# Attention beside a Fourier transform on one core: six tiles of exponentials instead of seven, and the turn of the maxima in another burst

## The chip, the cores and the metric

The kernel runs on one core of a Trainium2 chip. A core has a matrix engine (TensorE, in the profile PE, its weight loads PEld), VectorE (DVE), ScalarE (ACT), GpSimd (POOL) and SyncE (SP), which here only issues DMAs. The time is that of one execution on the device, in microseconds (us); "before" is the median of three runs.

## The reference

`x` is 2048 x 640, all in float32.

```python
g = sigmoid((x * gate_w).sum(-1, keepdims=True))
# a: attention with 32 heads of 20
q, k, v = split(x @ wqkv)
a = softmax(q @ k.T * 20 ** -0.5) @ v            # per head
a = merge_heads(a) @ wo
# b: Fourier mixing, real part
b = dft_seq_re @ (x @ dft_hid_re.T) - dft_seq_im @ (x @ dft_hid_im.T)
out = g * a + (1 - g) * b
```

## The kernel before

Attention is cut into 32 units: 16 pairs of heads by two halves of the queries. A unit has 32 steps, 1024 steps in all. Step `i` takes 128 keys and 512 queries for both heads of the pair: two score matmuls on PE ("e", transposed scores, into a PSUM bank each), two exponentials on ACT (L1123) into one tile `[128, 2, 512]`, and later the products with V on PE (L739), which add into the bank `av`. Softmax needs each query's maximum beforehand. So PE also computes plain scores ("m", L201), 43 steps ahead, and DVE reduces them (L203). When a unit's last m is done, `max_nm` (L218) makes the negated maxima `nm`, and `turn_max` transposes them on PE (L239), splits them on DVE into `m`, stores that to `m_scr` (L244) and loads it as two more rows of the queries `qst` (L250), so that the maxima are subtracted inside the e matmul. Store and load are handed to SP at the start of a step (`at_step`): 1 and 3 steps later.

The steps are grouped in cycles, and a table of letters sets PE's order inside a cycle: e and m are scores, F is a share of the other work (the Fourier transforms and the output product), B is the burst, in which the V products of all steps of the cycle run back to back. There are 56 cycles of 4 steps with the hidden transform; then the sequence transform (56 units of PE work, 672 steps), in which six of every eight units stand over two cycles of 6 steps (table `THIRDS`, "long") and two over three cycles of 4 (`SEQUENCE`, "short"), so 84 long and 42 short ones; then cycles of 4 with the output product. A unit of attention is 32 steps, so the ends of units recur in a pattern of 96 steps, 18 cycles.

The last pair of e in a cycle belongs to the first step of the next one. So a long cycle has seven live tiles of exponentials before its burst: five `p` buffers (`pair_tile`), one tile `p2`, and one lent by the pool `raw` of three buffers, which holds data from DRAM for POOL to split. The two extra tiles stand in `spares` and are taken in turn, two of every seven steps. In the sequence transform `raw` holds the chunks of the DFT matrix (`load_c`, L679, two of them at times; a second operand goes to `raw2`), which POOL adds (L685) and splits (L135, L136) into `part`; in the last of the seven products also a slab of the output weights (`wos`, L835).

All engines follow an order written by this program, in order; SP also issues its DMAs in order, so one that waits holds those behind it. PSUM banks for scores are five, taken in turn by `bank()`. An `E` in a table is an e whose score is computed at its place, but whose exponential (and whose step's start, `begin`) is kept in `held` until the burst's first product has been issued. `burst` also runs up to two of the queued `extras` (reading out a finished transform, adds, stores).

Of the kernel before, what the change touches and what calls it, by code (L numbers as in the profile page):

```python
# [34 lines left out]

HIDDEN = "emeFFmeFFFmeFFFmeFFmeFeFFFmFemmB", {"e": (0, 0, 1, 1), "m": (1, 1, 0, 1)}
SEQUENCE = "emeFmFFFFemFeFFmeFFemFFFmmFFFmeeB", {"e": (0, 0, 1, 1), "m": (1, 1, 1, 1)}
THIRDS = "emFemeFFFFmeFFmFeFmFFeFmeFFFmeFFmeFFmeFFFmFmmFeeB", {"e": (0, 1, 0, 1, 0, 1), "m": (1, 0, 1, 0, 1, 1)}
OUTPUT = "emFeFmFemeFFmeFFmeFFmFmFeFmeB", {"e": (1, 0, 0, 1), "m": (0, 1, 1, 0)}
LATE = "eeeeFFFFFFeeeEB", {"e": (0, 0, 0, 0), "m": (0, 0, 0, 0)}  # L40

# [52 lines left out]
def mix_kernel(ctx: ExitStack, tc: tile.TileContext, xa, xh, wqk, wb, wr, cdft, wo, out):  # L94
# [4 lines left out]
    def pools(**kw):  # L99
        return ctx.enter_context(tc.tile_pool(**kw))  # L100
# [44 lines left out]
    def bank():  # L145
        return ps_w.tile([P, 512], F32, name=f"ps{free[0][next(turn) % len(free[0])]}")
# [6 lines left out]
    def pair_tile():  # L153
        return work.tile([P, 2, 512], F32, name="p", bufs=5)

    def raw_tile():
        return work.tile([P, 1024], F32, name="raw", bufs=3)
# [8 lines left out]
    def load_stack(p):  # L166
        for t, o, parts in ((kst[p % 2], D, (0, 1, 0)), (qst[p % 2], 0, (0, 0, 1))):
            for h in range(2):
                r = o + (2 * p + h) * DH
                for k, z in enumerate(parts):  # L170
                    b = 64 * h + k * DH
                    yield (f32(t[b : b + DH, :]).rearrange("r (t c) -> r t c", t=4),
                           qk_scr[z, :, r : r + DH, :].rearrange("t r c -> r t c"))

    def q_unit(n):
        u = n % 2 * (S // 2)
        return qst[n // 2 % 2][:, u : u + S // 2]

    steps = [0]
    mx, nms, ends = {}, {}, []  # L180
# [6 lines left out]
    def at_step(i, fn):  # L187
        later.setdefault(i, []).append(fn)


    def s_mm(i, h):
        n, s = divmod(i, 32)
        if n >= NU:
            return lambda: None
        qt, kc = divmod(s, 4)
        q, k = q_unit(n), kst[(n // 2) % 2]
        if n not in mx:
            mx[n] = small.tile([P, 2, 8, 4], F32, name="mx", bufs=2)
        ps = bank()
        b = 64 * h  # L200
        pe.matmul(ps, q[b : b + KROWS, qt * P : (qt + 1) * P],  # L201
                  k[b : b + KROWS, kc * 512 : (kc + 1) * 512], start=True, stop=True)
        return lambda: dve.tensor_reduce(mx[n][:, h, qt, kc : kc + 1], ps, axis=AX.X, op=ALU.max)  # L203

    def s_end(i):
        n, s = divmod(i, 32)
        if n < NU and s == 31:
            if now[0] < 0:
                max_nm(n)
            else:  # L210
                ends.append(n)
        if s == 1 and 0 < n <= NU and now[0] < 0:
            turn_max(n - 1)

    def max_nm(n):
        nms[n] = small.tile([P, 32], F32, name="nm", bufs=2)
        m = mx.pop(n).rearrange("p h q (o c) -> p o (h q) c", o=1).to_broadcast([P, 2, 16, 4])
        dve.tensor_reduce(nms[n].rearrange("p (o k) -> p o k", o=2), m, axis=AX.X, op=ALU.max, negate=True)  # L218
# [118 lines left out]
    def flush(keep=0):  # L337
        while len(stores) > keep:
            sp.dma_start(*stores.pop(0))
# [329 lines left out]
    cparts, pts = {}, {}  # L669
# [63 lines left out]
    def av_step(i, n, kt):  # L733
        v = vts[n // 2]
        pp = [pts.pop((n, kt, qc)) for qc in range(2)]
        for qc in range(2):
            for h in range(2):
                j = 2 * qc + h
                pe.matmul(av[32 * j : 32 * j + DH + 1, :], v[:, kt, h * (DH + 1) : (h + 1) * (DH + 1)],  # L739
                          pp[qc][:, h, :], start=kt == 0, stop=kt == NS - 1)  # L740
        if kt == NS - 1:
            unit_end(i, n)
# [195 lines left out]
    def run_extras(g, most):  # L938
        while extras and most and extras[0][0] <= now[0]:
            extras.pop(0)[1]()  # L940
            most -= 1
        if more(g):
            n = g // (HT * NS) + 1
            preps.append((now[0] + 4, load_a(n, made.setdefault(n, 0))))
            made[n] += 1
        if preps and preps[0][0] <= now[0]:
            preps.pop(0)[1]()
# [7 lines left out]
    def start_dft():  # L955
        flush()
        wide.release()
        apool.append(pools(name="apool", bufs=1))
        spares.append(raw_tile().rearrange("p (z c) -> p z c", z=2))
        spares.append(apool[0].tile([P, 2, 512], F32, name="p2"))  # L960
        make_sel()
    ops = {}
# [2 lines left out]
    def make_sel():  # L965
        sel = apool[0].tile([P, P], F32, name="sel")
        for j in range(4):
            c = 32 * j + DH
            pool.tensor_copy(sel[:, 32 * j : 32 * j + 32], ident[:, c : c + 1].to_broadcast([P, 32]))
        chain.append(sel)  # L970
# [16 lines left out]
    HID = 8 * len(FEATURE)  # L987
# [9 lines left out]
    for u in range(UNITS):  # L997
        c = len(steps) - 1
# [7 lines left out]
    for u in range(2 * len(PRE)):  # L1006
        n = 2 if u >= 2 * len(PRE) - SLOW else 1
# [6 lines left out]
    def plan(c):  # L1014
        if HID <= c < outs_at:
            return THIRDS if steps[c + 1] - steps[c] == 6 else SEQUENCE
        return LATE if c >= late else OUTPUT if c >= outs_at else HIDDEN
# [9 lines left out]
    for k, tt in enumerate(PRE):  # L1027
        i = steps[tiles[2 * k]]
# [13 lines left out]
    def begin(i):  # L1042
        now[0] = i
        n, s = divmod(i, 32)
        for fn in later.pop(i, ()):
            fn()
        if s % 2 == 0:
            flush()
        if s == 0 and n % 2 == 0:
            p = n // 2  # L1050
            if p + 1 < NP:
                at_step(i + 6, functools.partial(load_v, p + 1))
            if 0 < p < NP - 1:
                for j, args in enumerate(load_stack(p + 1)):
                    at_step(i + 2 + j, functools.partial(sp.dma_start, *args))
        if i < total:
            k = (i - steps[HID]) % 7 - 5
            pts[n, s // 2, s % 2] = spares[k] if k >= 0 and steps[HID] < i <= steps[outs_at] else pair_tile()

    def end(i):  # L1060
        if i % 4 == 2:
# [28 lines left out]
    held, newest, spares = [], [], []  # L1090
    seen_ = const.tile([1, 1], F32, name="seen")

    def score(kind):
        hold, kind = kind == "E", kind.lower()
        x = heads[kind]
        heads[kind] += 1
        i, z = divmod(x, 2)
        h = z
        first, goes = plan(at_cycle[0])[1][kind], x - (2 * LEAD if kind == "m" else 0) - 2 - 2 * steps[at_cycle[0]]
        h ^= first[goes // 2 % len(first)]  # L1100
        if kind == "m":
            s_mm(i, h)()
            if z:
                s_end(i)
            if goes == 9 and len(first) == 6:
                pass_ends()
            return
        if z == 0 and i <= total and not hold:
            begin(i)
        if i < total:  # L1110
            n, s = divmod(i, 32)
            kt, qc = divmod(s, 2)
            q, k = q_unit(n), kst[(n // 2) % 2]
            b = 64 * h
            pt = bank()
            pe.matmul(pt, k[b : b + KROWS + 2, kt * P : (kt + 1) * P],  # L1116
                      q[b : b + KROWS + 2, qc * 512 : (qc + 1) * 512], start=True, stop=True)

            def exp():
                if z == 0 and hold:  # L1120
                    begin(i)
                newest[:] = [pts[n, kt, qc][:, h]]
                act.activation(newest[0], pt, AF.Exp, scale=float(DH) ** -0.5)  # L1123
                if z:
                    end(i)
                if goes == 2 * len(first) - 3:
                    while copies:
                        copies.pop()()

            held.append(exp) if hold else exp()  # L1130

    turned = []

    def pass_ends():
        for n in ends:
            max_nm(n)
        turned.extend(ends)
        ends.clear()

    def burst(c):  # L1140
        run_extras(max(done - HIDS, 0) // 3, 3 if c <= HID else 2)
        for n in ends:
            max_nm(n)
        for kt in range(steps[c] // 2, steps[c + 1] // 2):
            av_step(now[0], kt // NS, kt % NS)
            while turned:
                turn_max(turned.pop(0))
            while held:
                held.pop(0)()
        turned[:] = ends  # L1150
        ends.clear()
        if steps[c + 1] < total:
            act.activation(seen_, newest[0][0:1, 0:1], AF.Copy)
        if c == HID - 1:
            start_dft()
# [142 lines left out]
```

## Time and profile before

| | us |
|---|---|
| median of three runs | 1842.54 |
| lowest, highest | 1838.28, 1844.77 |
| the profiled execution | 1844.79 |
| its span | 1843.0 |
| hidden transform, first burst to last | 235.11 to 573.02 |
| sequence transform | to 1638.68 |
| output product, then the tail | to 1812.60, to 1843.0 |

"Busy" is the time in which an engine executes; time with a wait is not counted. Rows of a timeline give start, duration, engine, line, operation, output <- input, shapes, count, and in brackets the idle time before it with what ended it.

### The profile page before, as it was taken

What the parts mean: (1) busy time and instruction counts of PE and PEld (TensorE: products, weight loads), DVE (VectorE), ACT (ScalarE), POOL (GpSimd) and SP (SyncE); (2) the same over time, 40 slices, a digit from 0 to 9 for tenths busy, and PEclk for the clock granted to TensorE, in tenths of its full rate; (3) what the DMA queues carried; (4) which work ended last, traced back from release to release, by engine and by line L of the source; (5) the groups of instructions that cost most, each with busy time, mean ns of one, the idle gap of its engine ahead of it and who ended that gap; (6) DMA issues with size and microseconds to landing.
All of it is one profiled execution on the core that took longest, in us unless ns stands there. A gap on an engine that the chain in (4) does not pass through costs nothing. (4 is left out here: it accounts for less than half of the span.)

```text
span 1843.0 us, 45446 instructions
## 1 busy us (share of the span) xinstructions
PE 1818.7 (99%) x17917; PEld 1323.8 (72%) x17917; DVE 1425.6 (77%) x2427; ACT 1264.5 (69%) x2590; POOL 1303.7 (71%) x1104
## 2 busy tenths in 40 slices
PE   9999999999997999999999999999999999999998
PEld 7988876767675777777777777777777776676666
DVE  4157489888886888888788888888888887789953
ACT  4233377777775777777677777777777776677786
POOL 1379735666689788557779999967889987824444
PEclk9999999999998999999999999999999999999999
DMA  7899954877775574545576777556485856542224
GB/s 237 193 325 367 330 178 137 229 222 220 243 215 183 181 231 135 149 127 165 179 197 215 205 215 228 166 169 189 149 229 180 238 153 178 173 102 79 63 55 158
DMA packets 196009, 349.60 MB, mean 190 GB/s; under 512 B 54239, under 2 KB 107615, under 8 KB 194003
## 3 DMA queue, kind: packets, MB, share of 16 engines
q1 hardware_dynamic: 194515, 341.45, 61.3%
q0 software_dynamic: 1280, 5.25, 1.3%
q8 instruction: 141, 2.31, 0.5%
q14 instruction: 73, 0.60, 0.1%
HBM read 257.79 MB, written 88.65 MB: 188 GB/s over the span
## 5 line engine op out<-in xcount | busy, mean ns | idle before, releaser
L203 DVE TENSOR_REDUCE mx<-ps 128x1 f32<-128x512 f32 x2048 | 1269.6, 684 | 243.9 <-PE ps L201 208.5
L1123 ACT ACTIVATE p<-ps 128x512 f32<-128x512 f32 x1856 | 993.4, 601 | 359.2 <-PE ps L201 203.5
L201 PE MATMUL ps<-kst,qst 60*128 60x512 f32 x2048 | 747.6, 404 | 12.6 <-ACT raw L1123 9.4
L1116 PE MATMUL ps<-qst,kst 62*128 62x512 f32 x2048 | 717.2, 407 | 4.1 <-DMA qst<-m_scr 4.1
L827 PE MATMUL yp<-x,part 64*128 64x320 f32 x5376 | 661.8, 307 | 0.0
L827 PEld LDWEIGHTS yp<-x,part 64*128 64x128 f32 x5376 | 603.3, 186 | 8.1
L739 PE MATMUL av<-p,v 128*21 128x512 f32 x3712 | 486.5, 598 | 0.0
L1116 PEld LDWEIGHTS ps<-qst,kst 62*128 62x128 f32 x2048 | 340.2, 185 | 199.9 <-issue 77.7
L201 PEld LDWEIGHTS ps<-kst,qst 60*128 60x128 f32 x2048 | 345.8, 184 | 25.9 <-ACT raw L1123 9.7
L136 POOL TENSOR_TENSOR part<-raw,part 128x1024 fp32r<-128x1024 f32 (+3 forms) x134 | 296.7, 2214 | 10.2
L739 PEld LDWEIGHTS av<-p,v 128*21 128x21 f32 x3712 | 98.1, 101 | 202.3 <-issue 193.1
L518 PE MATMUL yp<-wb,x 64*128 64x320 f32 x1680 | 211.4, 306 | 0.0
L685 POOL TENSOR_TENSOR raw<-raw,raw 128x1024 f32<-128x1024 f32 x78 | 188.2, 2413 | 23.6 <-DMA raw<-in_cdft 17.6
L135 POOL CAST part<-raw 128x1024 fp32r<-128x1024 f32 (+2 forms) x127 | 125.0, 984 | 111.3 <-PE yp L827 79.6
L518 PEld LDWEIGHTS yp<-wb,x 64*128 64x128 f32 x1680 | 194.2, 186 | 2.5
L1123 ACT ACTIVATE raw<-ps 128x512 f32<-128x512 f32 x192 | 107.5, 599 | 49.0 <-PE ps L201 25.8
L739 PE MATMUL av<-raw,v 128*21 128x512 f32 x384 | 99.9, 599 | 0.0
L898 PE MATMUL yp<-x,part 64*128 64x320 f32 x720 | 92.5, 311 | 0.0
L531 POOL TENSOR_TENSOR x<-x,raw 128x640 f32<-128x640 f32 x40 | 62.6, 1564 | 41.8 <-DVE raw L528 37.9
L714 POOL TENSOR_TENSOR araw<-araw 128x320 f32<-128x320 f32 x80 | 70.1, 876 | 30.3 <-DMA araw<-a_scr 29.0
L136 POOL TENSOR_TENSOR x<-araw,x 128x320 fp32r<-128x320 f32 x96 | 84.0, 875 | 7.7
L898 PEld LDWEIGHTS yp<-x,part 64*128 64x128 f32 x720 | 80.3, 186 | 1.6
(117 smaller groups left out, 1507.9 us busy)
## 6 DMA issues: line engine op xcount, KB each, us to landing
raw<-in_cdft SPq DMA_DIRECT2D x188, 512.0 KB
araw<-a_scr SPq DMA_DIRECT2D x176, 160.0 KB
qk_scr<-p SPq DMA_DIRECT2D x40, 512.0 KB
kst<-qk_scr SPq DMA_DIRECT2D x90, 160.0 KB
w_scr<-wb SPq DMA_DIRECT2D x36, 400.0 KB
qst<-qk_scr SPq DMA_DIRECT2D x90, 160.0 KB
wb<-w_scr SPq DMA_DIRECT2D x8, 1600.0 KB
part<-in_xh SPq DMA_DIRECT2D x10, 1024.0 KB
```

The costliest lines, as they stand in the source:

```text
L135: e1.tensor_copy(dst1, src)
L136: e2.tensor_tensor(dst2, src, f32(dst1), op=ALU.subtract)
L201: pe.matmul(ps, q[b : b + KROWS, qt * P : (qt + 1) * P], k[b : b + KROWS, kc * 512 : (kc + 1) * 512], start=True, stop=True)
L203: return lambda: dve.tensor_reduce(mx[n][:, h, qt, kc : kc + 1], ps, axis=AX.X, op=ALU.max)
L518: pe.matmul(ps[z], lefts[n][a][r, d, k * P : k * P + P], rights[2 * n + hf][r, b, d], start=done_ == 0, stop=done_ == 3 * ND - 1)
L685: pool.tensor_tensor(raws[0], raws[0], raws[1], op=ALU.add if PRODUCTS[n][0][1][0] > 0 else ALU.subtract)
L714: pool.tensor_tensor(raws[0], raws[0], raws[1], op=ALU.add if PRODUCTS[n][1][1][0] > 0 else ALU.subtract)
L739: pe.matmul(av[32 * j : 32 * j + DH + 1, :], v[:, kt, h * (DH + 1) : (h + 1) * (DH + 1)], pp[qc][:, h, :], start=kt == 0, stop=kt == NS - 1)
L827: pe.matmul(yp[h][:, :HE], c[r, cz, cs], a[r, az], start=s == 0 and z == 0, stop=s == NS - 1 and z == 2)
L898: pe.matmul(yp[h][:, :HE], o[r, oz, d], wos[d, hf][r, wz], start=d == 0 and z == 0, stop=d == ND - 2 and z == 2)
L1116: pe.matmul(pt, k[b : b + KROWS + 2, kt * P : (kt + 1) * P], q[b : b + KROWS + 2, qc * 512 : (qc + 1) * 512], start=True, stop=True)
L1123: act.activation(newest[0], pt, AF.Exp, scale=float(DH) ** -0.5)
```

## The change

The step ahead of a long cycle is no longer exponentiated before that cycle's burst, but inside it, after the first product (the letters `EE`). Six tiles then do: five `p` and `p2`, which is taken at every sixth step; the pool `raw` keeps its three buffers. And a unit's maxima that end in a long cycle are no longer reduced and queued in mid-cycle (`pass_ends`, after the tenth m, if they had ended by then). `burst` reduces them at its start and turns them after its last product; in a short cycle the turn comes in the next burst, as before.

```diff
-THIRDS = "emFemeFFFFmeFFmFeFmFFeFmeFFFmeFFmeFFmeFFFmFmmFeeB", {"e": (0, 1, 0, 1, 0, 1), "m": (1, 0, 1, 0, 1, 1)}
+THIRDS = "emFemeFFFFmeFFmFeFmFFeFmeFFFmeFFmeFFmeFFFmFmmFEEB", {"e": (0, 1, 0, 1, 0, 1), "m": (1, 0, 1, 0, 1, 1)}
...
-        spares.append(raw_tile().rearrange("p (z c) -> p z c", z=2))
         spares.append(apool[0].tile([P, 2, 512], F32, name="p2"))
...
-            k = (i - steps[HID]) % 7 - 5
-            pts[n, s // 2, s % 2] = spares[k] if k >= 0 and steps[HID] < i <= steps[outs_at] else pair_tile()
+            spare_ = steps[HID] < i <= steps[outs_at] and (i - steps[HID]) % 6 == 5
+            pts[n, s // 2, s % 2] = spares[0] if spare_ else pair_tile()
...
-            if goes == 9 and len(first) == 6:
-                pass_ends()
...
-    def pass_ends():
-        for n in ends:
-            max_nm(n)
-        turned.extend(ends)
-        ends.clear()
-
     def burst(c):
         run_extras(max(done - HIDS, 0) // 3, 3 if c <= HID else 2)
         for n in ends:
             max_nm(n)
-        for kt in range(steps[c] // 2, steps[c + 1] // 2):
+        kts = range(steps[c] // 2, steps[c + 1] // 2)
+        if len(kts) > 2:
+            turned.extend(ends)
+            ends.clear()
+        for kt in kts:
             av_step(now[0], kt // NS, kt % NS)
-            while turned:
+            while turned and (len(kts) == 2 or kt == kts[-1]):
                 turn_max(turned.pop(0))
             while held:
                 held.pop(0)()
-        turned[:] = ends
+        turned.extend(ends)
         ends.clear()
```

In the built program three places show it. First ACT's queue at the end of the first long cycle (the numbers behind names tell buffers' uses apart; `o` is the unit's result copied out of `av`). Before:

```order
L1123 ACTIVATE p_8739<-ps0_8752 128x512
L1123 ACTIVATE raw_8654<-ps2_8762 128x512
L1123 ACTIVATE raw_8654<-ps4_8772 128x512
L1128 ACTIVATE o_8646<-av_97 128x512
L1123 ACTIVATE p2_8655<-ps3_8802 128x512
L1123 ACTIVATE p2_8655<-ps4_8805 128x512
L1153 ACTIVATE seen_2691<-p2_8655 1x1
```

And now:

```order
L1120 ACTIVATE p_8738<-ps0_8751 128x512
L1120 ACTIVATE p2_8654<-ps2_8761 128x512
L1120 ACTIVATE p2_8654<-ps4_8771 128x512
L1125 ACTIVATE o_8646<-av_97 128x512
L1120 ACTIVATE p_8814<-ps3_8794 128x512
L1120 ACTIVATE p_8814<-ps4_8796 128x512
L1148 ACTIVATE seen_2691<-p_8814 1x1
```

The sixth step's exponentials go to `p2` instead of the lent `raw`, and the seventh's to a `p` that the burst frees; ACT's order is the same here.

Second PE's queue in a burst that turns a unit's maxima (the fourth long cycle of the sequence transform). Before:

```order
L1116 MATMUL ps1_9278<-qst1_94,kst1_92 128x512
L739 MATMUL av_97<-p_9117,v_6185 21x512 x2
L739 MATMUL av_97<-raw_8654,v_6185 21x512 x2
L239 MATMUL ps2_9294<-ident_86,nm_9261 32x32 x4
L739 MATMUL av_97<-p2_8655,v_6185 21x512 x2
L739 MATMUL av_97<-p_9188,v_6185 21x512 x2
L739 MATMUL av_97<-p_9210,v_6185 21x512 x2
L739 MATMUL av_97<-p_9238,v_6185 21x512 x2
L1116 MATMUL ps3_9313<-qst1_94,kst1_92 128x512
```

And now:

```order
L1113 MATMUL ps1_9275<-qst1_94,kst1_92 128x512
L739 MATMUL av_97<-p_9132,v_6185 21x512 x2
L739 MATMUL av_97<-p_9144,v_6185 21x512 x2
L739 MATMUL av_97<-p_9163,v_6185 21x512 x2
L739 MATMUL av_97<-p_9190,v_6185 21x512 x2
L739 MATMUL av_97<-p_9212,v_6185 21x512 x2
L739 MATMUL av_97<-p2_8654,v_6185 21x512 x2
L239 MATMUL ps2_9303<-ident_86,nm_9286 32x32 x4
L1113 MATMUL ps3_9316<-qst1_94,kst1_92 128x512
```

The four transposes move from behind the first of three products (four matmuls each) to behind the last. In the unit of every three whose last m stands in the last place of a long cycle, they move from this place in the burst after to that in the cycle's own burst. Nothing else in PE's order changes.

Third SP's queue in the last product of the sequence transform, where output weights are loaded too. Before:

```order
L835 DMA raw_24890<-in_wo 128x640
L244 DMA m_scr_85<-m_25018 128x64
L679 DMA raw_25042<-in_cdft 128x1024
L679 DMA raw2_25044<-in_cdft 128x1024
L835 DMA raw_25055<-in_wo 128x640
L769 DMA r_scr_81<-lc_24395 128x16
L931 DMA y_scr_80<-yt_24561 128x320
L250 DMA qst1_94<-m_scr_85 1x32x32 x4
```

And now:

```order
L835 DMA raw_24960<-in_wo 128x640
L931 DMA y_scr_80<-yt_24629 128x320
L244 DMA m_scr_85<-m_25096 128x64
L679 DMA raw_25114<-in_cdft 128x1024
L679 DMA raw2_25116<-in_cdft 128x1024
L835 DMA raw_25127<-in_wo 128x640
L769 DMA r_scr_81<-lc_24462 128x16
L250 DMA qst1_94<-m_scr_85 1x32x32 x4
```

The store of a transform's sum (`y_scr`) stands one step earlier, ahead of the maxima's store; such stores move so in many places, since `burst` counts their eight steps from a step that has not yet begun. The loads keep their order, with three buffers of `raw` to take instead of two.

## The prediction

> **What bounds the kernel now.** I read the page first: who is busy, and what clock TensorE was granted.
>
> ```profile
> PE 1818.7 (99%) x17917; PEld 1323.8 (72%) x17917; DVE 1425.6 (77%) x2427; ACT 1264.5 (69%) x2590; POOL 1303.7 (71%) x1104
> ...
> PEclk9999999999998999999999999999999999999999
> ```
>
> PE is busy for 99% of the span, so no engine but PE sets the time, and a change that leaves PE's instructions alone can win only PE's few idle microseconds and the time spent at a lower clock. The clock dips in the 13th of 40 slices. Next I read whom PE waited for.
>
> ```profile
> PE ps L201 <- ACT raw L1123: 9.4, 1, 9.4
> PE ps L1116 <- DMA qst<-m_scr: 4.1, 3, 2.0
> PE ps L201 <- DMA qst<-qk_scr: 2.7, 1, 2.7
> ```
>
> Five waits, 16.2 us, and each falls in the DFT stage whose buffers the change rearranges. To price them with what follows them, I took stretches of whole cycles (from the start of one AV burst to the start of a later one) that hold a wait, and beside each a stretch with the same place in the repeating pattern of long and short cycles and no wait. Columns: the stretch, its length, busy time (and count) of each engine, granted clock, DMA share, GB/s.
>
> ```profile
> 573.02:602.25 29.23, 19.85 (x187) 13.85 (x185) 15.35 (x26) 13.49 (x27) 25.16 (x24) 0.82 0.58 193
> 640.58:658.25 17.67, 17.67 (x187) 13.23 (x185) 15.02 (x26) 13.58 (x27) 17.09 (x14) 1.00 0.87 243
> 872.80:895.13 22.33, 20.66 (x202) 13.92 (x201) 15.39 (x29) 14.06 (x28) 14.94 (x11) 0.92 0.44 132
> 723.52:742.22 18.70, 18.70 (x203) 13.54 (x201) 15.41 (x29) 14.06 (x28) 10.29 (x9) 1.00 0.56 152
> 1324.39:1334.56 10.17, 9.70 (x106) 6.90 (x104) 8.41 (x17) 6.72 (x14) 7.93 (x7) 1.00 0.50 155
> 723.52:732.91 9.39, 9.39 (x106) 6.83 (x104) 7.64 (x16) 6.70 (x13) 5.62 (x6) 1.00 0.33 90
> 1528.44:1537.02 8.58, 6.62 (x66) 4.61 (x64) 6.32 (x11) 4.45 (x10) 5.95 (x7) 1.00 0.41 119
> 1378.94:1385.20 6.26, 6.26 (x66) 4.43 (x64) 5.06 (x10) 4.44 (x9) 5.97 (x8) 1.00 0.67 187
> 1560.95:1573.29 12.34, 9.67 (x98) 6.91 (x96) 7.99 (x15) 6.89 (x14) 12.04 (x8) 1.00 0.84 244
> 1409.12:1418.40 9.28, 9.28 (x99) 6.71 (x97) 7.81 (x14) 6.89 (x14) 8.99 (x8) 1.00 0.55 168
> ```
>
> The counts of PE agree within one in each pair, so the differences are pure loss: 29.23 - 17.67 = 11.56 us, 22.33 - 18.70 = 3.63, 10.17 - 9.39 = 0.78, 8.58 - 6.26 = 2.32, 12.34 - 9.28 = 3.06. Together 21.35 us. In the first two pairs the loss is larger than PE's idle time in the row (9.38 and 1.67), because the granted clock fell to 0.82 and 0.92. The clean stretches show no idle PE at all, so in steady state nothing is to be won.
>
> **The lent raw tile (term 1, 11.56 us).** The one long wait, engine by engine:
>
> ```profile
> 590.46 0.79 PE L201 MATMUL ps<-kst,qst 60*128 60x512 f32 x1 [9.38 <-ACT raw L1123]
> 589.81 1.09 ACT L1123 ACTIVATE raw<-ps 128x512 f32<-128x512 f32 x2 [9.97 <-POOL part L136]
> 568.50 2.41 POOL L136 TENSOR_TENSOR part<-wb,part 128x1024 fp32r<-128x1024 f32 x1
> 583.92 2.34 POOL L685 TENSOR_TENSOR raw<-raw,raw 128x1024 f32<-128x1024 f32 x1 [2.73 <-DMA raw<-in_cdft]
> 587.44 2.34 POOL L136 TENSOR_TENSOR part<-raw,part 128x1024 fp32r<-128x1024 f32 x1
> ```
>
> The first exponential into the lent tile needs one of three raw buffers; the first to come free holds a DFT matrix chunk, which POOL reads until 587.44 + 2.34 = 589.78, and the exponential starts at 589.81. The PSUM banks stay full behind it and PE stops for want of one. After the change that step goes to the tile `p2`, whose memory POOL last read in the row at 568.50, over at 570.91, ten microseconds before the exponential wants it; the next step is held and takes the tile that the burst's first product releases. Nothing in the first long cycle waits for a raw tile. POOL's add of the last hidden-transform product moves ahead of the chunk's sum, into the 2.73 us in which POOL idles for the chunk's DMA; an add of nearly that size would still fit. Next late is POOL's chunk for the second DFT unit: finished at 589.78 as before, and needed when PE has done the two cycles of the clean row (17.67) and the burst behind them, 573.02 + 17.67 + 2.7 = 593.4. So 3.6 us of cover are left, and I take the whole 11.56; the ends are 11.56 and, if POOL's chain came late by as much as one more chunk (2.34 + 2.34 plus its cast, about 6 us), 9.
>
> **The turn of the maxima (term 2, 3.63 + 0.78 us).** Every third unit's maxima end in the last score pair of a long cycle, too late for the mid-cycle call, and are turned one burst later.
>
> ```profile
> 874.45 0.32 SPq L244 DMA_DIRECT2D m_scr<-m  x1
> 877.92 2.71 SPq L250 DMA_DIRECT2D qst<-m_scr  x4
> 883.61 0.59 PE L1116 MATMUL ps<-qst,kst 62*128 62x512 f32 x2 [1.67 <-DMA qst<-m_scr]
> ```
>
> The four loads are out at 880.63 and PE gets its rows 3.0 us later, 1.67 too late. Turned at the end of the burst before, this chain starts a long cycle earlier (9.3) less the two products that now stand ahead of the turn (2 x 0.9): about 7.5 us earlier, which covers 1.67. So 4.41 us go. The other two units in three are turned in the same burst as now, but behind all three products:
>
> ```profile
> 774.83 2.70 SPq L250 DMA_DIRECT2D qst<-m_scr  x4
> 783.25 0.40 PE L1116 MATMUL ps<-qst,kst 62*128 62x512 f32 x2
> ```
>
> Their turn moves back by 1.8 us, and the store by 0 to 1.8. SP works in order, so the chunk loads and the maxima's loads queued behind the store slip with it. Those loads end at 777.53, land by some 780.5 (the 3.0 us from above), and are needed at 783.25: 2.7 us of cover, 0.9 or more after. Cost zero; with the cover gone, at most 1.8 us for each of 14 units, 25 us.
>
> **The third raw tile (term 3, 2.32 + 3.06 us).** In the last DFT product three raw tiles are wanted at once (two chunks and a slab of the output weights) and two are there.
>
> ```profile
> 1524.57 2.11 SPq L679 DMA_DIRECT2D raw<-in_cdft  x2
> 1530.52 0.33 SPq L835 DMA_DIRECT2D raw<-in_wo  x1
> 1532.24 2.73 SPq L250 DMA_DIRECT2D qst<-m_scr  x4
> 1561.85 0.83 SPq L679 DMA_DIRECT2D raw<-in_cdft  x2
> 1563.20 1.00 SPq L1046 DMA_DIRECT2D qst<-qk_scr  x2
> 1528.11 2.38 POOL L136 TENSOR_TENSOR part<-raw,part 128x1024 fp32r<-128x1024 f32 x1
> 1512.15 0.87 POOL L925 TENSOR_TENSOR yt<-yt,m 128x320 f32<-128x320 f32 x1
> 1531.37 0.43 SPq L931 DMA_DIRECT2D y_scr<-yt  x1
> ```
>
> SP stands from 1526.7 until POOL's read ends at 1530.49, with the maxima's loads behind it; those come 1.96 us late (8.58 - 6.62 in the row above). It stands again until 1561.85, with the last two loads of the next queries behind it; those come 2.67 late. A free third tile takes 3.8 us from the first, of which the later store takes back at most 1.8, and several such stands from the second. Ends: 0 (SP finds another wait in its place) and 5.38; I take 5.38, since both margins exceed the waits.
>
> **The held exponentials.** PE's scores keep their order; only ACT's two exponentials, and the loads and stores that SP is handed at that step's start, move behind the burst's first product. None of the loads of maxima above is due at a held step; of the next pair's keys and queries one or two in twelve are, 0.9 us later, and term 3 has several to spare. A steady burst:
>
> ```profile
> 714.16 1.92 PE L739 MATMUL av<-p,v 128*21 128x512 f32 x16
> 716.86 0.50 PE L1116 MATMUL ps<-qst,kst 62*128 62x512 f32 x1
> 714.27 1.09 ACT L1123 ACTIVATE p<-ps 128x512 f32<-128x512 f32 x2 [0.59 <-PE ps L1116]
> 717.40 1.09 ACT L1123 ACTIVATE p<-ps 128x512 f32<-128x512 f32 x2 [1.66 <-PE ps L201]
> 716.12 0.28 DVE L218 TENSOR_REDUCE nm<-mx 128x32 f32<-128x128 f32 x1
> ```
>
> The burst issues for 2.70 us, 0.9 a product. The pair starts at 714.16 + 0.9 = 715.06 instead of 714.27 and ends at 716.15; ACT then idles till 717.40, 1.66 us before and about 0.9 now. Cost zero. Ends: zero (PE never waited here, so no gain), and, if the pair could start only when the burst is through (716.86 + 1.09 = 717.95), 0.55 us in each of 84 long cycles, 46 us. The release is the first product's, so I stay at zero. The negated maxima are ready at 716.40, the turn comes at 716.86: no wait either.
>
> **Sum.** 11.56 + 4.41 + 5.38 = 21.35. The profiled execution took 1844.79 us (span 1843.0), 2.25 above the median of 1842.54; 1844.79 - 21.35 = 1823.4. I forecast 1823.
>
> [...]
>
> ```profile
> 884.10:887.50 3.40, 3.40 (x21) 0.85 (x24) 0.49 (x1) 1.48 (x4) 3.25 (x3) 0.53 0.86 246
> ```
>
> Here 1.67 idle microseconds were followed by 3.4 us at about half clock. [...]
>
> **Rivals.** (a) Terms 1 and 2 go, term 3 stays, because SP finds the next wait (a `y_scr` store now stands a step earlier in its queue and waits for POOL): 1844.79 - 15.97 = 1828.8. For it: SP has many waits in that stage. Against: POOL had added this one up at 1513.02 (the row of L925), and its store was issued at 1531.37, 18 us behind; a place earlier is 1.5 of them. (b) At the start of the DFT stage POOL becomes late instead, since PE arrives 9.4 us sooner: one chunk of 6 us less the cover of 3.6 gives 2.4 back, twice at most: 1826 to 1828. (c) The other side: the held pair stands at the head of ACT's queue, and everything behind it stands too. If it is released late, the next long cycle starts short of PSUM banks. It decides from 21.35 / 84 = 0.25 us a long cycle; at 0.55 the time is 1823.4 + 46 = 1870. Against it stand ACT's 0.9 idle us. [...] (d) The lent tile's wait merely moves to `p2`, and nothing is won: 1842.
>
> **Chances.** Forecast 0.66, (a) 0.13, (b) 0.13, (c) 0.05, (d) 0.03. The runs of before spread over 6.5 us, and the lowest, 1838.28, less the sum gives 1817; (a) with some of (b) reaches 1831. Range 1817 to 1831. About 0.3% (5.5 us) is what a measurement of this kernel can tell: faster 0.93, same 0.03, slower 0.04.
>
> **What would show it.** Right: no PE wait above 2 us in the DFT stage, PEclk 9 in the 13th slice, no `raw` written by the exponentials, SP's wait of L835 gone, long cycles still 9.25 to 9.4. Wrong: long cycles 0.2 or more longer with PE waiting for ACT (c); PE waiting for POOL's `part` near 590 us (b); waits for `qst` near 1520 to 1560 us (a).

## The result, and the profile after

1822.94 us (median of six runs, 1821.64 to 1823.93) against 1842.47 before (six runs, 1838.28 to 1848.48): ratio 0.9891, 95% interval 0.9874 to 0.9909. The profiled execution of the changed kernel took 1822.32 us, its span 1820.5. The head of its page:

```profile
PE 1813.4 (100%) x17917; PEld 1332.4 (73%) x17917; DVE 1422.7 (78%) x2427; ACT 1275.6 (70%) x2590; POOL 1304.3 (72%) x1104
...
PEclk9999999999999999999999999999999999999999
```

The dip in the 13th slice is gone. Whom PE waited for, the whole answer:

```profile
PE ps L304 <- DVE x L298: 1.5, 1, 1.5
PE ps L201 <- ACT p L379: 0.5, 1, 0.5
PE ps L349 <- ACT x L133: 0.3, 1, 0.3
```

All three stand in the loading and projection stage. The sequence transform, from its first cycle to its last burst, took 1616.22 - 571.68 = 1044.54 us against 1638.68 - 573.02 = 1065.66, so 21.1 us went there. (The profiled executions lie 1844.79 - 1822.32 = 22.5 us apart, the medians 19.5; single executions of the kernel before spread over 10.2 us, of the changed kernel over 2.3.) The five stretches of the prediction, the same cycles by number (the third row pairs with 1324.39:1334.56):

```profile
571.68:589.38 17.70, 17.70 (x187) 13.27 (x185) 15.24 (x26) 13.61 (x28) 15.84 (x18) 1.00 0.68 226
860.09:878.70 18.61, 18.61 (x194) 13.46 (x192) 15.02 (x27) 14.30 (x28) 17.40 (x12) 1.00 0.61 180
1308.11:1317.42 9.31, 9.31 (x98) 6.74 (x96) 7.34 (x14) 6.83 (x14) 8.47 (x7) 1.00 0.76 224
1511.18:1517.45 6.27, 6.27 (x67) 4.46 (x65) 5.07 (x10) 4.44 (x9) 2.58 (x5) 1.00 0.51 171
1541.45:1550.73 9.28, 9.28 (x98) 6.69 (x97) 7.72 (x14) 7.07 (x14) 8.99 (x6) 1.00 0.69 206
```

17.70, 18.61, 9.31, 6.27 and 9.28 us, where there were 29.23, 22.33, 10.17, 8.58 and 12.34: each at full clock, without idle PE, and within 0.1 us of its clean partner. A long burst of the changed kernel that turns maxima, in the timeline of PE, ACT and DVE:

```profile
608.00 2.77 PE L739 MATMUL av<-p,v 128*21 128x512 f32 x24
610.59 0.24 PE L239 MATMUL ps<-ident,nm 128*32 128x32 f32 x8
609.15 1.08 ACT L1120 ACTIVATE p<-ps 128x512 f32<-128x512 f32 x2 [0.95 <-PE av L739]
611.29 2.28 ACT L1120 ACTIVATE p<-ps 128x512 f32<-128x512 f32 x4 [0.83 <-PE ps L201]
609.61 0.28 DVE L218 TENSOR_REDUCE nm<-mx 128x32 f32<-128x128 f32 x1
```

The held pair starts 1.15 us into the burst, released by the first product, and ACT still idles 0.83 us before the next cycle's first exponential. The negated maxima are ready at 609.89, PE turns them at 610.59.

One sign that the prediction named did not come whole: SP's wait for the slabs of the output weights (L835) is not gone. Before, then now:

```profile
SPq L835 <- POOL part L136: 22.4, 5, 5.7
```

```profile
SPq L835 <- POOL part L136: 3.2, 1, 3.2
```

No wait of PE follows from it.

### The profile page after: what moved, and what is told of

Same layout as the page of the kernel before. It is cut to its first block, busy times and chain, and to the rows that moved or that the text cites. A ratio compares the mean times of both kernels' runs of the same rounds, so it can differ in the third digit from the quotient of the medians.

```text
span 1820.5 us, 45577 instructions
## 1 busy us (share of the span) xinstructions
PE 1813.4 (100%) x17917; PEld 1332.4 (73%) x17917; DVE 1422.7 (78%) x2427; ACT 1275.6 (70%) x2590; POOL 1304.3 (72%) x1104
## 5 line engine op out<-in xcount | busy, mean ns | idle before, releaser
L1120 ACT ACTIVATE p<-ps 128x512 f32<-128x512 f32 x2048 | 1093.3, 600 | 357.2 <-PE ps L201 160.1
L136 POOL TENSOR_TENSOR part<-raw,part 128x1024 fp32r<-128x1024 f32 (+3 forms) x134 | 297.4, 2219 | 10.2
L915 POOL TENSOR_TENSOR x<-x,m 128x320 f32<-128x320 f32 x30 | 26.2, 874 | 79.4 <-DVE m L910 72.8
L925 POOL TENSOR_TENSOR yt<-yt,m 128x320 f32<-128x320 f32 x64 | 55.4, 877 | 13.5 <-DVE m L847 13.5
```

The source lines that it names most:

```text
L136: e2.tensor_tensor(dst2, src, f32(dst1), op=ALU.subtract)
```

## The experiments

My theory was that three independent terms make up the gain: the first use of the lent tile (11.56), the place of the turn (4.41) and the third raw tile in the last product (5.38). The first rival was that they are one thing, the lent tile. Each kernel was run beside the kernel before on one chip; ratios are to that.

**The turn alone.** The kernel before, with the new `burst` and without `pass_ends`:

```diff
+        if len(kts) > 2:
+            turned.extend(ends)
+            ends.clear()
...
+            while turned and (len(kts) == 2 or kt == kts[-1]):
                 turn_max(turned.pop(0))
```

> The kernel before with the new turn alone (seven tiles, one still lent by raw). Three independent terms: only term 2 goes, 4.4 us off 1842.5, so about 1838; the 9.4 us wait for the lent tile stays, no PE wait for the maxima's rows is left in the first six products, and the waits of the last product stay, that for the maxima's rows perhaps up to 1.8 us longer since its turn is later. Rival, the lent tile is behind everything: the maxima still come late because SP stands for raw tiles, about 1842. Rival, the later turn costs in the other 14 units: up to 25 us more, about 1860.

1842.59 us against 1844.54; ratio 0.9987 (the 95% interval, here and below in brackets, is 0.9973 to 1.0). That is 2 us, at the edge of what the runs can tell, where I expected 4.4. It is the time of the first rival (1842); its mechanism holds in part. PE's waits say where the rest went:

```profile
PE ps L201 <- ACT raw L1121: 9.6, 1, 9.6
PE ps L1114 <- DMA qst<-m_scr: 4.2, 1, 4.2
```

The waits of every third unit (1.67 and 0.47) are gone, as expected and against the rival. But the wait in the last product has grown from 1.96 to 4.17, and the clock now fell behind it:

```profile
1533.50:1540.40 6.90, 6.35 (x30) 2.82 (x32) 1.12 (x2) 2.37 (x5) 6.09 (x4) 0.51 0.74 215
```

By the bursts' starts, this wait cost 7.4 us over two cycles instead of 2.3. The wait for queries (2.7 us before) is no longer in the list, and its stretch lost 0.4 us instead of 3.1: PE starts that stretch 0.4 us later than before (1561.38), and the loads go out 2.0 us earlier (1561.25 against 1563.20). SP's rows show the chain (with one gap):

```profile
1519.92 0.33 SPq L244 DMA_DIRECT2D m_scr<-m  x1
1522.25 0.81 SPq L679 DMA_DIRECT2D raw<-in_cdft  x2
1528.20 0.33 SPq L835 DMA_DIRECT2D raw<-in_wo  x1
...
1529.90 2.78 SPq L250 DMA_DIRECT2D qst<-m_scr  x4
```

The store was issued at 1519.92, but the load of the weights' slab stood until a raw tile came free at 1528.2, and the maxima's loads behind it until 1529.90. The lateness of the store does not set this. The tile came free when POOL had read its chunk, at 1528.18 (1530.49 before). PE's burst there began at 1523.77 (1528.44 before), so against PE that read ended at 4.41 us instead of 2.05, and the 2.36 us between them cover the 2.2 us by which the wait grew. The other kernel with the new turn and a lent tile (below) shows the same, 4.58, and its twin with the old turn does not, 2.37. So the new turn costs here as long as SP stands for a tile; why POOL then comes later against PE no run isolates.

**The six tiles alone.** The changed kernel with the old turn (`pass_ends` and the old `burst`), run on two chips, the second time beside the changed kernel.

```diff
+            if goes == 9 and len(first) == 6:
+                pass_ends()
...
-        if len(kts) > 2:
-            turned.extend(ends)
-            ends.clear()
...
-            while turned and (len(kts) == 2 or kt == kts[-1]):
+            while turned:
                 turn_max(turned.pop(0))
```

> The changed kernel with the old turn (maxima reduced in mid-cycle, or turned one burst later where they end too late). Three independent terms: terms 1 and 3 are kept and term 2 comes back, about 1823 + 4.4 = 1827, with PE waiting for the maxima's rows once in three units by up to 2 us. Rival: with a third raw tile SP issues the maxima's loads earlier by itself, so the old turn costs nothing, 1823.

> The changed kernel with the old turn, again. If the new turn is worth nothing once the third raw tile is free, it equals the changed kernel within 2 us; if it is worth term 2 of the prediction, it is 4.4 us slower; what the first trace shows (one wait of 0.72 us) would make it 1 us slower.

> The changed kernel again, beside the next kernel on one chip: 21 us below the kernel before.

First 1824.51 us, ratio 0.9886 (0.9868 to 0.9905); then 1824.49, ratio 0.9891 (0.9877 to 0.9905), beside the changed kernel's 1822.74, ratio 0.9882 (0.9868 to 0.9896). The intervals overlap, but the runs of the two on that one chip, four each, do not (1824.01 to 1824.91 and 1822.32 to 1823.00). With six tiles, the new turn is worth 1.75 us, not 4.4. Of the maxima's waits the second trace has one, where 0.47 us were waited before (the first trace has 0.72 us there), and by the bursts' starts its cycle is 1.6 us longer than in the changed kernel:

```profile
PE ps L1115 <- DMA qst<-m_scr: 1.2, 1, 1.2
```

The place that waited 1.67 us before does not wait, though its turn stands where it stood. SP's rows there, first of the kernel before, then of this one:

```profile
874.45 0.32 SPq L244 DMA_DIRECT2D m_scr<-m  x1
875.21 2.00 SPq L679 DMA_DIRECT2D raw<-in_cdft  x2
```

```profile
863.01 0.32 SPq L244 DMA_DIRECT2D m_scr<-m  x1
863.43 0.85 SPq L679 DMA_DIRECT2D raw<-in_cdft  x2
864.33 0.42 SPq L819 DMA_DIRECT2D yt<-y_scr  x1
864.85 2.73 SPq L250 DMA_DIRECT2D qst<-m_scr  x4
```

Before, the two chunk loads between store and loads took 2.00 us, since one stood for a raw tile; with three raw tiles they take 0.85 and start sooner. The maxima's loads follow their store by 1.84 us instead of 877.92 - 874.45 = 3.47. That 1.6 us is the wait of 1.67.

**The lent tile one cycle later.** The kernel before, with the first long cycle alone holding its step ahead, so that `raw` is first written in the second; the old turn, and then the new one too.

```diff
+        if c == HID:
+            return THIRDS[0].replace("FeeB", "FEEB"), THIRDS[1]
...
-            k = (i - steps[HID]) % 7 - 5
+            k = 1 if i == steps[HID + 1] - 1 else (i - steps[HID + 1]) % 7 - 5 if i >= steps[HID + 1] else -1
```

> The kernel before, in which the first long cycle alone holds the exponentials of its step ahead, so that the lent raw tile is first written one long cycle later; seven tiles with one lent and the old turn from then on. Three independent terms: term 1 alone goes, 11.6 us, about 1831, and the waits for maxima and queries stay. Rival: the first wait shifts PE against the DMAs and is behind the later waits too, about 1823. Rival: POOL is late next, since PE comes 9.4 us sooner, about 1833 to 1840.

> The same with the new turn: all of the change but the third raw tile from the second long cycle on. Three independent terms: only term 3 is missing, 1823 + 5.4 = 1828.4, with PE waiting for maxima and queries in the last product of the sequence transform. Rival: the waits of the last product come from the order on SP's queue and not from the tiles, then 1823.

With the old turn 1835.91 us, ratio 0.995 (0.9935 to 0.9966): 8.6 us, where I expected 11.6 and the rival with a late POOL had 1833 to 1840. PE's waits of that kernel:

```profile
PE ps L1118 <- DMA qst<-m_scr: 5.1, 3, 2.1
PE ps L201 <- DMA o_scr<-o: 2.6, 1, 2.6
...
PE ps L201 <- ACT raw L1125: 1.3, 1, 1.3
```

The lent tile is still waited for, 1.3 us in the second long cycle, since POOL's read of the chunk ends no earlier (587.99 + 2.38 = 590.37 here): this much that rival had right. By the bursts' starts that leaves 1.9 of the 11.5 us; the missing microsecond (9.6 saved there, 8.6 in all) went in other places, 3.4 us at half clock after the 2.6 us wait among them. The waits for maxima and queries are all there, so they are no consequence of the first wait. With the new turn 1832.62 us, ratio 0.9934 (0.9916 to 0.9951), where I expected 1828.4: the third units no longer wait, and the wait in the last product is 4.3 us at

```profile
1523.20:1530.00 6.80, 5.54 (x24) 2.00 (x26) 0.31 (x1) 1.63 (x4) 6.58 (x5) 0.50 0.68 198
```

half clock, 7.2 us over two cycles. Take this and 1.7 us of the first use off the median and the changed kernel is left: 1832.6 - 8.9 = 1823.7.

**How much the held pair may be late.** Extra copies on ACT behind the held pair, two or six:

```diff
+            dumps = 2 if held else 0
             while held:
                 held.pop(0)()
+            for _ in range(dumps):
+                act.activation(dump_, newest[0][:, :128], AF.Copy)
```

> The changed kernel with two extra copies of 128 columns on ACT behind the held pair in each of the 84 long bursts, about 0.5 us of ACT's time (they write a tile of their own and change no result). ACT idled 0.83 us there, so the cover holds: within 2 us of the changed kernel. Rival, the held pair already sits on the edge: up to 0.5 us a long cycle, 42 us slower.

> The changed kernel with six extra copies on ACT behind the held pair (they write a tile of their own and change no result): two took 0.65 us and left 0.28 us of idle ACT, so six take about 1.8 and overrun the cover by 0.9 us in each of 84 long bursts. If the price were the overrun itself, as the rival of the prediction had it, 75 us slower, 1898. If the five PSUM banks and ACT's slack later in the cycle (it is busy for about 7 us of 9.3) take it up, less than 0.2 us a long cycle, under 17 us slower.

Two: 1823.44 us, ratio 0.9886 (0.9869 to 0.9903), against the changed kernel's 0.9882, no difference; the copies take 0.65 us and 0.28 of idle ACT is left. Six: 1915.91 us, ratio 1.0384 (1.0367 to 1.0401). That is 93 us slower than the changed kernel by the ratios. My own bet, under 17 us, was wrong, and the rival's 75 came nearer.

```profile
713.71 2.02 ACT L1148 ACTIVATE dump<-p 128x128 f32<-128x128 f32 x6
715.73 5.53 ACT L1121 ACTIVATE p<-ps 128x512 f32<-128x512 f32 x10
```

```profile
PE ps L201 <- ACT p L1121: 40.6, 84, 0.8
```

PE waits in each of the 84 long cycles, and these get about 0.95 us longer (9.26 to 10.24 where nothing else happens), for 2.02 us of copies over 0.83 of cover: 0.95 paid for an overrun of 1.19. The profile shows only half of this as waiting (40.6 us over 84 cycles); the rest lies in stretches in which PE counts as busy. Nine of the last ten cycles hold one exponential too (the table `LATE` has an `E`, before as well), so they also got the copies and some 12 us of the loss. PSUM banks and ACT's later slack gave back little, 0.24 us a cycle.

**Where in the burst the turn may stand.** The changed kernel with the turn behind the first product, or the second:

```diff
-            while turned and (len(kts) == 2 or kt == kts[-1]):
+            while turned:
```

```diff
-            while turned and (len(kts) == 2 or kt == kts[-1]):
+            while turned and (len(kts) == 2 or kt == kts[1]):
```

> The changed kernel with the turn behind the first product of the same burst instead of the last. The negated maxima are ready 1.5 to 1.9 us into the burst and PE comes to the turn at 0.9: 0.6 to 1.1 us of waiting in each of 21 bursts, about 20 us slower than the changed kernel, 1843. Rival, PE's pipeline hides so short a wait: within 3 us of the changed kernel, since the loads of the maxima then come earlier.

> The changed kernel with the turn behind the second product. The negated maxima are ready 1.5 to 1.9 us into the burst and PE comes to the turn at 1.75: between no wait and 0.2 us in 14 of the 21 bursts, so within 3 us of the changed kernel. If a late semaphore or the weight load made any nearness costly, 5 to 10 us slower.

First: 1842.26 us, ratio 0.9989 (0.9979 to 0.9998), 19.5 us slower than the changed kernel, all of the gain.

```profile
PE ps L239 <- DVE nm L218: 15.9, 21, 0.9
```

Second: 1825.27 us, ratio 0.9892 (0.9873 to 0.9911), 1.8 us slower by the ratios (0.9892 - 0.9882 = 0.001), which their intervals don't separate; in the trace the cycles that turn maxima are 0.25 and 0.2 us longer, for two units in three, 14 cycles and about 3 us in all.

## Why the prediction was right, point by point

The time came out at 1823 as forecast. The sum (21.35) is the loss of the profiled execution, and there the sequence transform became 21.1 us shorter; another 1.34 us of the 22.5 lie ahead of it, where the change does nothing. One of the sum's terms stood on half of its cause.

- **Term 1, the lent tile, 11.56: right.** The stretch went from 29.23 to 17.70. POOL's chunk was ready at 589.94 (forecast 589.78) and needed at 589.38 + 2.77 = 592.15 (forecast 593.4); the cover of 2.2 us held, so rival (b) did not come. Delaying the first use by one long cycle showed that the wait is on this one chunk: it leaves 1.3 us of it. Nothing waits for `p2` (rival (d)); its margin is nine microseconds and not ten, since the exponential was wanted from 589.81 - 9.97 = 579.84 on and POOL was through at 570.91.
- **Term 2, 3.63 + 0.78 to the new turn: the stretches right, the cause half right.** The step that failed is that these 4.41 us hang on the turn alone, "too late for the mid-cycle call, and are turned one burst later". The waits were the sum of a late turn and an SP that stood for a raw tile between store and load (the row at 875.21, which I had read over). Either part of the change removes them without the other, the turn wholly, the six tiles all but a wait of 0.7 to 1.2 us. With the tiles in place the turn is worth 1.75 us.
- **"Cost zero" for the other 14 units: right in the changed kernel, wrong by itself.** In the two kernels with the new turn and a lent tile the wait in the last product was 4.17 and 4.31 us, in the two with the old turn 1.96 and 2.09, and a loss of 2.3 became 7.4 and 7.2. How the later turn does this stays open; the store that it delays is not what the loads stood for.
- **Term 3, 5.38: right as a sum, mis-sized as a part.** With the new turn and a lent tile the last product loses 7.2 to 7.8 instead of 5.38. So the terms are not independent: the turn alone won 2 us and not 4.41, since it made the loss in the last product larger. That 2 and 20 us for the two parts alone come near the 21 of both is no sign of independence.
- **The held pair, zero: right.** ACT's idle time went to 0.83 where I said 0.9; the pair starts 1.15 us into the burst where I said 0.9. Rival (c) did not come, but its mechanism and its price are real: the six copies show that most of an overrun is paid, 0.95 us of 1.19.
- **The turn behind the last product waits for nothing: right**, and the margin was real: two products earlier it costs 19.5 us, one earlier about 3 us in the trace, too little for the times to separate.
- The store of `y_scr` that moved ahead (rival (a)) cost nothing that shows: PE has no wait left there, though SP still stands 3.2 us for one slab.

## What to carry to other kernels

The buffer borrowed from a pool of transfers was paid for twice here: at its first use, when POOL was still reading it, and later by a DMA queue that stood in order for the pool and held back loads that have nothing to do with it. Before crediting a late load to where its data are made, read what stands between its store and its load on the queue. And before moving work of an engine later, read its idle time at the place where it rejoins: here 0.83 us was there, 0.65 us more work cost nothing, and 2.02 us more cost 0.95 in every long cycle.

## What the runs showed of the hardware

How a wait of PE went with half clock, in the sequence transform of all traces: about 3.4 us of half clock after waits of 1.67 us (the kernel before), 1.70 and 2.57 us (the lent tile one cycle later, with the old turn), but none after 1.96 and 2.67 (the kernel before) and 2.09 (the lent tile one cycle later), and none after 1.34 us or less; 6.83 us with 4.17 and 4.31 (the two kernels with the new turn and a lent tile), 10.24 us with 9.38 and 9.63 (the kernel before and the turn alone). The longer stretches began inside the wait: in the kernel before, the clock was at half from 583.94 to 594.18, and PE stood until 590.46, so only 3.7 us of its work were slowed. My estimate from these figures is that such a wait cost its length and half of the work that ran at half clock: 9.38 + 3.72 / 2 = 11.2 of the 11.5 us that its stretch lost, and 1.67 + 3.41 / 2 = 3.4 of 3.6. A shorter wait was followed by half clock once: in the output product of the kernel with six copies, 0.91 us (until 1869.25) was followed by half clock from 1871.58 to 1874.99, while an equal one twelve microseconds later was followed by none.

The lengths measured, 3.4, 6.83 and 10.24 us, are near one, two and three times 3.41. In the trace of the kernel before, the changes of clock at 583.94, 594.18, 884.31 and 887.73 lie 10.24, 290.13 and 3.42 us apart, 3, 85 and 1 times 3.413. The length of a wait alone did not decide between 1.7 and 2.7 us: 1.67, 1.70 and 2.57 us were followed by half clock, 1.96, 2.09 and 2.67 were not. What does decide, and why one wait of 0.91 us was followed by half clock and the other was not, no run here shows.
